# Attention of a soft mixture-of-experts kernel in 64x64 tiles of the matrix unit

## The chip, the cores and the metric

The kernel runs on one core of a Trainium2 chip. The metric is the device time of one execution in microseconds (us). Engines are named as the profile names them: PE is the matrix engine (PEld its weight loads), DVE the vector engine, ACT the scalar engine, POOL the general engine, SP the engine that only issues DMAs.

## The reference, cut to what matters

```python
def _attn_ref(q, k, v):                 # each (8, 12, 448, 64): batch, heads, tokens, head size
    scores = scale * np.matmul(q, k.transpose(0, 1, 3, 2))
    m = np.max(scores, axis=-1, keepdims=True)
    e = np.exp(scores - m)
    attn = e / (np.sum(e, axis=-1, keepdims=True) + np.exp(-m) + 1e-09)
    return np.matmul(attn, v)
...
def _moe_ref(x, phi, w1, w2):           # x (3584, 768); phi (768, 32); 8 experts of 768 x 1024 x 768
    logits = x @ phi
    d = softmax of logits over the rows; slot_input = d.T @ x
    slot_out = per expert: relu(slot_input[e] @ w1[e]) @ w2[e]
    c = softmax of logits over the slots
    return c @ slot_out
```

The first part is attention for 96 heads with one more term in the denominator, the second a soft mixture of experts over all 3584 rows that the attention gives.

## The kernel before, in words

The attention works on 48 pairs of heads (`NPAIR`), one after the other. A pair sits on the 128 partitions, 64 for each head. Six pairs are a batch element, three pairs a load group. Each pair goes through these steps; the line numbers are those of the profile.

- `load` (L168) brings q, k and v of three pairs with DMAs that POOL issues and that convert to bf16. q and k come with both heads on the partitions, one DMA each (L176). v comes in two DMAs (L180, L181), four of a partition's seven tokens each, so that one token is read twice, and `V` (L406) sorts it into place with four POOL copies.
- `T` (L241) turns q and k with 28 transposes of 64x64 (L256) into a PSUM bank of the pool psB; ACT (L263) or DVE (L265) copies the result.
- `A` (L274) makes the scores with queries as output rows, three chunks of 128 queries per head and a last chunk where the 64 remaining queries of both heads share a bank. DVE takes the maximum of each row (L287, L298, L307).
- `W1`, `W2`, `W3` (L310, L332, L340) turn the maxima of a group of three pairs into rows (`mT`): W1 writes the negated maxima on POOL, W2 are four products on PE, W3 copies the result with ACT and takes the exponential of the negated maximum.
- `Bk` (L352) makes the scores again, now with keys as output rows, adds the negated maxima by a product with a selection matrix, and ACT takes the exponential (L372, L402). In its mixed form it has one chunk of A woven in: a, b, b, bias, bias, a.
- `AV` (L421) multiplies by v, with a column of ones for the sum: per key chunk six products of 128x128 and two of 128x64, 65 columns each (L436), into one bank of the pool psV.
- `N1` (L443) evacuates that bank (ACT, L449), `N2` (L452) divides: two small operations on DVE (L464, L465), then three on POOL (L469, L479, L480).
- `PX` (L494) turns the pair's x with four 128x128 products (L501), ACT copies it (L507).
- `P` (L516) is the batch element's part of the mixture: logits, maxima, exponentials and the sums over the rows, in six steps that `post` spreads over the slots after the batch.

There are seven key chunks' worth of exponentials and seven reduces for a pair, each 128x448. The order is written out by hand: the program's order is the order of every engine's queue. The first pairs follow the list `ramp` (L716). Then the loop at L758 runs a slot for each pair in two halves (y = 0, 1): scores of pair s with the maxima of a later pair woven in, AV of pair s and s-1, turns of pair s+6, x of pair s-2. W1 is issued in the first half of every third slot (L805), ahead of the weight loads, and N2 of the pair before only in the second half (L803); W2 and W3 follow the turns in the second half (L783, L784). In the slots POOL also issues the loads of the experts' weights, half a matrix at a time (`load_half`, `half_at`), and later rows of them (`load_rows`, `stage_rows`).

PSUM has eight banks: three for A and P (psA), four for the scores of Bk, the turns and x (psB), one for AV (psV). After the attention come the experts' two products and the output, which the change hardly touches.

Of the kernel before, what the change touches and what calls it, by code (L numbers as in the profile page):

```python
# [24 lines left out]
HG = 6  # L25
NP = 3
W65 = 65
VS = 66
# [3 lines left out]
def kernel(  # L32
# [37 lines left out]
    ident2 = const.tile([128, 128], BF16, name="ident2")  # L70
    ones = const.tile([128, 2], BF16, name="ones")
    sel = const.tile([128, HG], BF16, name="sel")
    phi_sb = const.tile([128, KC, NS], BF16, name="phi_sb")
    halfm = const.tile([128, 2], F32, name="halfm")
    nhalfm = const.tile([128, 2], F32, name="nhalfm")
    band = const.tile([128, 4], BF16, name="band")

    NQK, NE, VPN, NATV = 7, 5, HG * 4 * VS, HG * 4 * D  # L80
    sizes = [("nq0", 2 * NP * S), ("nq1", 2 * NP * S), ("nv", NATV), ("qk6", 2 * S), ("wm1", 512),
             ("qk0", 2 * S), ("qk1", 2 * S), ("qk2", 2 * S), ("wm0", 512), ("xTa", 4 * 512), ("qk3", 2 * S),
             ("vp0", VPN), ("x0", 4 * DD), ("qk4", 2 * S), ("qk5", 2 * S), ("e2", NE * 2 * S), ("e1", S),
             ("vp1", VPN), ("xTb", 2 * 512), ("x1", 4 * DD)]
# [10 lines left out]
    e2_t = [part("e2", i * 2 * S, 2 * S).rearrange("p (h s) -> p h s", h=2) for i in range(NE)]  # L95
    e1_t = part("e1", 0, S)
    vp = [part(f"vp{i}", 0, VPN).rearrange("p (h i d) -> p h i d", h=HG, i=4) for i in range(2)]
    wm = [part(f"wm{i}", 0, 512).rearrange("p (i c) -> p i c", i=4) for i in range(2)]
# [57 lines left out]

    with ExitStack() as at:
# [4 lines left out]
        psB = pool("psB", 4, space=PSUM)  # L162
# [3 lines left out]
        ubuf = pu.tile([128, 2, 7 * W65], F32, name="ubuf")  # L166

        def load(g, nm, l0=0, l1=NP):  # L168


            b, h0 = g // 2, (g % 2) * HG
            src = {"q": q, "k": k, "v": v}[nm][b, h0:h0 + HG]
            if nm != "v":
                t = part(f"nq{g % 2}", "qk".index(nm) * NP * S, NP * S).rearrange("p (l x) -> p l x", l=NP)
                x = src.rearrange("(l h) (j t) d -> (h j) l (t d)", h=2, t=7)
                gdma(out=t[:, l0:l1, :], in_=x[:, l0:l1, :])  # L176
            else:
                t = part("nv", 0, NATV).rearrange("p (h t d) -> p h t d", h=HG, t=4)
                x = src.rearrange("h (p t) d -> p h t d", t=7)
                gdma(out=t[0:64], in_=x[:, :, 0:4, :])  # L180
                gdma(out=t[64:128], in_=x[:, :, 3:7, :])  # L181
            nat[nm, g] = t
# [3 lines left out]
        for a, src in enumerate((q, k)):  # L186
            nc.sync.dma_start(out=raw[:, a, :], in_=src[0, 0:2].rearrange("h (j t) d -> (h j) (t d)", t=7))
# [9 lines left out]
        for t in wm:  # L197
            nc.vector.memset(t, 0.0)

        def ones_in(t, eng):  # L200

            eng.memset(t, 0.0)
            eng.memset(t[:, :, 0:3, D:W65], 1.0)
            eng.memset(t[0:64, 0:HG:2, 3, D:W65], 1.0)
            eng.memset(t[64:128, 1:HG:2, 3, D:W65], 1.0)

        ones_in(vp[0], nc.vector)
        for t, x in ((halfm, 1.0), (nhalfm, -1.0)):
            nc.vector.memset(t, 0.0)
            for hl in range(2):  # L210
                nc.vector.memset(t[64 - 64 * hl:128 - 64 * hl, hl:hl + 1], x)
        nc.vector.memset(ones, 1.0)
        nc.vector.memset(ones[64:128, 1:2], 0.0)
# [4 lines left out]
        for h in range(2):  # L218
            nc.vector.tensor_add(ident2[:, 64 * h:64 * h + 64], ident[:, 0:64], ident[:, 64:128])
# [11 lines left out]
        mx, ngm, ec, mT, eT, av, us = {}, {}, {}, {}, {}, {}, {}  # L231
        qkT = {}
        st = {"e2": 0}


        def kcol(hl, tok):
            if hl == 0:
                return 384 if tok == 0 else (tok - 1) * 128 if tok < 4 else (tok - 4) * 128 + 64
            return tok * 128 if tok < 3 else (tok - 3) * 128 + 64 if tok < 6 else 384

        def T(n):  # L241
            g, pl = divmod(n, NP)
            first = n < NP * NP
            ps = psB.tile([128, 2, S], BF16, tag="b", name="ps_t")

            k0 = [psB.tile([128, 2, S], BF16, tag="b", name="ps_k") for _ in range(2)] if n == 0 else None
            for a in range(2):
                src = nat["qk"[a], g]
                order = [(tok, hl) for tok in range(7) for hl in range(2)]
                if a and n == 0:  # L250
                    order.sort(key=lambda z: kcol(z[1], z[0]))
                for tok, hl in order:
                    c = kcol(hl, tok) if a else (2 * tok if tok < 4 else 2 * tok - 7) * 64
                    r = slice(64 * hl, 64 * hl + 64)
                    o = k0[c // 256][r, 0, c:c + 64] if a and n == 0 else ps[r, a, c:c + 64]
                    nc.tensor.transpose(o, src[r, pl, tok * D:(tok + 1) * D], ident[r, r])  # L256
            t = qk_t[n % NQK]
            if n == 0:
                nc.scalar.copy(t[:, 0, :], ps[:, 0, :])
                nc.vector.tensor_copy(t[:, 1, 0:256], k0[0][:, 0, 0:256])  # L260
                nc.vector.tensor_copy(t[:, 1, 256:S], k0[1][:, 0, 256:S])
            elif first or n % 6 in (1, 3):
                nc.scalar.copy(t, ps)  # L263
            else:
                nc.vector.tensor_copy(t, ps)  # L265
            qkT[n] = t
# [5 lines left out]
        mg, mpl = (lambda n: group[n][0]), (lambda m: (0, (firsts + [NPAIR])[m + 1] - firsts[m]))  # L272

        def A(n, i, steps=False):  # L274
            g, pl = group[n]
            if g not in mx:
                mx[g] = psm.tile([128, 21], F32, tag="mx", name="mx")
            t = qkT[n]
            if steps:
                m = mx[g]  # L280

                def run(hl):
                    r = slice(64 * hl, 64 * hl + 64)
                    ps = psA.tile([128, 512], F32, tag="a", name="ps_a")
                    nc.tensor.matmul(ps[:, 0:S], t[r, 0, i * 128:(i + 1) * 128], t[r, 1, :], start=True, stop=True)  # L285
                    c = HG * i + 2 * pl + hl
                    nc.vector.reduce_max(m[:, c:c + 1], ps[:, 0:S], axis=AX.X)  # L287

                return [lambda: run(0), lambda: run(1)]
            if i < 3:  # L290
                pss = [psA.tile([128, 512], F32, tag="a", name="ps_a") for _ in range(2)]
                for hl in range(2):
                    r = slice(64 * hl, 64 * hl + 64)
                    nc.tensor.matmul(pss[hl][:, 0:S], t[r, 0, i * 128:(i + 1) * 128], t[r, 1, :],  # L294
                                     start=True, stop=True)
                for hl in range(2):
                    c = HG * i + 2 * pl + hl
                    nc.vector.reduce_max(mx[g][:, c:c + 1], pss[hl][:, 0:S], axis=AX.X)  # L298
            else:
                ps = psA.tile([128, 512], F32, tag="a", name="ps_a")  # L300

                for hl in range(2):
                    r = slice(64 * hl, 64 * hl + 64)
                    nc.tensor.matmul(ps[64 - 64 * hl:128 - 64 * hl, 0:S], t[r, 0, 384:448], t[r, 1, :],  # L304
                                     start=True, stop=True)
                c = 3 * HG + pl
                nc.vector.reduce_max(mx[g][:, c:c + 1], ps[:, 0:S], axis=AX.X)  # L307


        def W1(g):  # L310
            w, m = wm[g % 2], mx[g]
            l0, l1 = mpl(g)
            nm = psm.tile([128, 21], BF16, tag="ngm", name="ngm")
            neg = lambda o, s: nc.gpsimd.tensor_scalar(o, s, -1.0, None, op0=ALU.mult)
            cols = lambda t: t[:, 0:3 * HG].rearrange("p (i c) -> p i c", i=3)[:, :, 2 * l0:2 * l1]

            o = w[:, 3, :].rearrange("p (d c) -> p d c", d=2)[:, :, 2 * l0:2 * l1]
            nc.gpsimd.tensor_mul(
                o.rearrange("p d (l h) -> p d l h", h=2),
                m[:, 3 * HG + l0:3 * HG + l1].unsqueeze(1).unsqueeze(3).to_broadcast([128, 2, l1 - l0, 2]),  # L320
                nhalfm.unsqueeze(1).unsqueeze(1).to_broadcast([128, 2, l1 - l0, 2]))
            o = w[:, 0:3, :].rearrange("p i (d c) -> p i d c", d=2)[:, :, :, 2 * l0:2 * l1]
            neg(o, cols(m).unsqueeze(2).to_broadcast([128, 3, 2, 2 * (l1 - l0)]))
            if l1 - l0 == NP:
                neg(nm, m)
            else:
# [705 lines left out]
```

## Time and profile before

| what | value |
|---|---|
| median of 3 runs | 297.94 us (297.47 to 299.71) |
| the profiled execution, from first to last instruction | 299.0 us |
| mean granted PE clock | 0.956 (1.00 until 260 us) |
| PE, DVE, ACT, POOL busy in 60 to 80 us, of 20 us | 19.96, 19.60, 19.64, 16.44 |
| first and last of the products of PX | 32.8 us, 253.0 us |
| DMA share in 60 to 80 us | 1.15 |

The profiled execution's own time is its span: the page gives no time outside it. It is 1.1 us over the median. A busy time is the time in which at least one instruction of the engine was under way; instructions overlap, so the distance between starts says what one costs. A DMA share above 1 means that packets of the 16 engines overlap. The queue "instruction" in the list of DMA queues carries the program's own code to the engines.

### The profile page before, as it was taken

What the parts mean: (1) busy time and instruction counts of PE and PEld (TensorE: products, weight loads), DVE (VectorE), ACT (ScalarE), POOL (GpSimd) and SP (SyncE); (2) the same over time, 40 slices, a digit from 0 to 9 for tenths busy, and PEclk for the clock granted to TensorE, in tenths of its full rate; (3) what the DMA queues carried; (4) which work ended last, traced back from release to release, by engine and by line L of the source; (5) the groups of instructions that cost most, each with busy time, mean ns of one, the idle gap of its engine ahead of it and who ended that gap; (6) DMA issues with size and microseconds to landing.
All of it is one profiled execution on the core that took longest, in us unless ns stands there. A gap on an engine that the chain in (4) does not pass through costs nothing.

```text
span 299.0 us, 12398 instructions
## 1 busy us (share of the span) xinstructions
PE 271.4 (91%) x5174; PEld 162.5 (54%) x5174; DVE 249.7 (84%) x581; ACT 249.8 (84%) x559; POOL 195.9 (66%) x391
## 2 busy tenths in 40 slices
PE   5999899999999999999899999999999999996820
PEld 4445456566666566566556666656665555652100
DVE  5899799999999989999889999998999675537930
ACT  3569999999899989998989899989999987337820
POOL 8792887979696979887879697978686633000000
PEclk9999999999999999999999999999999999997555
DMA  7999998999999999999999999999799989908997
GB/s 132 147 143 208 149 138 138 188 165 188 185 204 179 184 176 202 163 182 182 202 159 184 176 199 152 196 183 196 125 150 187 213 185 263 344 10 318 380 453 322
DMA packets 47015, 58.67 MB, mean 196 GB/s; under 512 B 2800, under 2 KB 39920, under 8 KB 46704
## 3 DMA queue, kind: packets, MB, share of 16 engines
q0 software_dynamic: 40304, 42.29, 89.6%
q1 hardware_dynamic: 6656, 15.60, 13.8%
q8 instruction: 40, 0.66, 0.8%
q14 instruction: 15, 0.12, 0.1%
HBM read 89.16 MB, written 15.14 MB: 349 GB/s over the span
## 4 chain that ended last, share of the span: by engine, by line
PE 68%; ACT 10%; DVE 6%; POOL 6%; issue 4%; DMA 2%; DVEq 0%; POOLq 0%; ACTq 0%
PE ps_av L436 15%; PE ps_a L285 10%; PE ps_b L367 7%; PE ps_b L370 7%; PE ps_t L256 5%; PE ps_b L396 5%; PE ps_x L501 3%; PE ps_b L399 3%; ACT W L402 2%; PE ps_o L925 2%; DVE mx L298 2%; PE ps_s L623 2%; PE ps_h L862 2%; PE ps_so L882 2%; ACT W L263 2%
## 5 line engine op out<-in xcount | busy, mean ns | idle before, releaser
L287 DVE TENSOR_REDUCE mx<-ps_a 128x1 f32<-128x448 f32 x250 | 137.3, 613 | 4.6 <-PE ps_a L285 3.5
L372 ACT ACTIVATE W<-ps_b 128x448 bf16<-128x448 f32 x250 | 120.4, 574 | 0.0
L285 PE MATMUL ps_a<-W 64*128 64x448 bf16 x250 | 80.9, 352 | 0.0
L367 PE MATMUL ps_b<-W 64*128 64x448 bf16 x250 | 70.5, 352 | 1.1
L436 PE MATMUL ps_av<-W 128*128 128x65 bf16 (+1 forms) x1536 | 64.9, 196 | 2.2 <-issue 1.6
L436 PEld LDWEIGHTS <-W 128*128 128x128 bf16 (+1 forms) x1536 | 50.5, 100 | 30.2 <-issue 26.4
L370 PE MATMUL ps_b<-mT,sel 64*128 64x448 bf16 x250 | 66.5, 350 | 0.0
L469 POOL TENSOR_TENSOR W<-ubuf,rec 128x384 bf16<-128x384 f32 x44 | 36.3, 824 | 35.7 <-ACT W L507 19.3
L402 ACT ACTIVATE W<-ps_b 128x448 bf16<-128x448 f32 x86 | 46.1, 574 | 2.0 <-PE ps_b L399 2.0
L256 PEld LDWEIGHTS <-W 64*64 64x64 bf16 x1344 | 29.3, 112 | 12.7 <-issue 4.3
L507 ACT CAST W<-ps_x 128x512 bf16<-128x512 f32 x47 | 28.6, 608 | 7.4 <-PE ps_x L501 7.2
L256 PE MATMUL ps_t<-ident,W 64*64 64x64 bf16 x1330 | 30.6, 195 | 2.4 <-ACT W L215 1.4
L307 DVE TENSOR_REDUCE mx<-ps_a 128x1 f32<-128x448 f32 x48 | 29.5, 615 | 1.4 <-PE ps_a L304 1.4
L285 PEld LDWEIGHTS <-W 64*128 64x128 bf16 x250 | 23.4, 94 | 9.8
L114 POOL DMA_DIRECT2D W<-in_moe_w_dram x30 | 22.6, 755 | 7.9 <-PE ps_b L399 7.8
L370 PEld LDWEIGHTS <-sel 64*128 64x128 bf16 x250 | 19.6, 94 | 14.4 <-issue 5.6
L396 PE MATMUL ps_b<-W 64*64 64x448 bf16 (+1 forms) x134 | 27.1, 374 | 0.3
L449 ACT COPY ubuf<-ps_av 128x455 f32<-128x455 f32 x44 | 25.1, 571 | 0.8 <-POOL W L408 0.6
L399 PE MATMUL ps_b<-mT,sel 64*64 64x448 bf16 (+1 forms) x134 | 25.1, 354 | 0.1
L263 ACT COPY W<-ps_t 128x896 bf16<-128x896 bf16 x21 | 19.5, 927 | 6.5 <-PE ps_t L256 6.5
L298 DVE TENSOR_REDUCE mx<-ps_a 128x1 f32<-128x448 f32 x38 | 21.1, 616 | 1.9 <-PE ps_a L294 1.9
L480 POOL TENSOR_TENSOR W<-ubuf,rec 128x128 bf16<-128x128 f32 x44 | 17.5, 398 | 3.7
(156 smaller groups left out, 446.6 us busy)
## 6 DMA issues: line engine op xcount, KB each, us to landing
W<-in_moe_w_dram POOLq DMA_DIRECT2D x24, 768.0 KB, 9.9
W<-in_v_dram POOLq DMA_DIRECT2D x32, 192.0 KB, 6.5
out_dram<-W SPq DMA_DIRECT2D x2, 2688.0 KB, 10.0
W<-in_q_dram POOLq DMA_DIRECT2D x15, 336.0 KB, 6.3
W<-in_k_dram POOLq DMA_DIRECT2D x15, 336.0 KB, 7.5
stage<-in_moe_w_dram POOLq DMA_DIRECT2D x4, 768.0 KB, 9.6
W<-stage SPq DMA_DIRECT2D x4, 576.0 KB, 7.3
out_dram<-W SPq DMA_DIRECT2D x6, 384.0 KB, 3.0
```

What stands on the lines that cost most here:

```text
L256: nc.tensor.transpose(o, src[r, pl, tok * D:(tok + 1) * D], ident[r, r])
L285: nc.tensor.matmul(ps[:, 0:S], t[r, 0, i * 128:(i + 1) * 128], t[r, 1, :], start=True, stop=True)
L287: nc.vector.reduce_max(m[:, c:c + 1], ps[:, 0:S], axis=AX.X)
L307: nc.vector.reduce_max(mx[g][:, c:c + 1], ps[:, 0:S], axis=AX.X)
L367: nc.tensor.matmul(pss[hl][:, 0:S], t[rs[hl], 1, cols], t[rs[hl], 0, :], start=True, stop=False)
L370: nc.tensor.matmul(pss[hl][:, 0:S], sel[rs[hl], 2 * pl + hl:2 * pl + hl + 1].to_broadcast([64, 128]), mT[mg(n)][rs[hl], :], start=False, s ...
L372: nc.scalar.activation(e[:, hl, :], pss[hl][:, 0:S], AF.Exp, scale=scale)
L396: nc.tensor.matmul(outs[hl], t[rs[hl], 1, cols], t[rs[hl], 0, :], start=True, stop=False)
L399: nc.tensor.matmul(outs[hl], sel[rs[hl], 2 * pl + hl:2 * pl + hl + 1].to_broadcast([64, m]), mT[mg(n)][rs[hl], :], start=False, stop=True)
L402: nc.scalar.activation(e, p[:, 0:S], AF.Exp, scale=scale)
L436: nc.tensor.matmul(o, eT[n, i, hl][:, qc], vp[g % 2][:, 2 * pl + hl, i, 0:W65], start=(i == 0 and u == 0 and hl == 0) or (u == 3 and i == ...
L469: eng.tensor_mul(x[:, 0:3, c:c + 128].rearrange("p i (h d) -> p i h d", h=2), u[:, 0:6, 0:D].rearrange("p (i h) d -> p i h d", h=2), rec[: ...
```

## The change

All products of the attention take the form of 64x64 tiles, so that the two halves of the rows and the two halves of the columns of the matrix unit can hold four products at once.

- Seven chunks of 64 keys (or queries) per head in place of three of 128 and one of 64. `M` replaces A: two products, output halves swapped, one reduce. `R_` replaces Bk: two score products, then one M, then two bias products, then one exponential of both heads together. One bank per chunk; psB has three banks.
- `AV`: per key chunk 16 products of 64x64 with 65 columns, the eight with swapped halves first. The output takes two banks, the only buffer of psV.
- `TP` replaces T and PX: 16 turns of x and 28 of q and k, all 64x64, into that same buffer of psV; k is loaded with the heads' halves swapped, by two DMAs.
- `W2` makes 8 products of 64 columns, `W3` gets its exponentials from 4 more products on PE. W1 is two POOL products.
- v comes in one DMA per group and is copied by one POOL operation; N2 is one POOL product instead of three operations.
- A slot is one sequence of seven chunks, with AV of the pair before behind chunks 1 to 3, N1 at 3, N2 at 4, TP at 5. W1, W2, W3 stand at the end of chunks 4, 5 and 6 of every third slot.
- One of the logit products gets an extra one (`twin`) that masks a doubled half; the row counts of the late weight loads move by one.

```diff
-        psB = pool("psB", 4, space=PSUM)
+        psB = pool("psB", 3, space=PSUM)
...
+            if nm == "k":
+                for h in range(2):
+                    gdma(out=t[rs[1 - h], l0:l1, :], in_=x[h, :, l0:l1, :])
...
+        def TP(n=None, m=None):
+            ps = psV.tile([128, 2, 1024], BF16, tag="v", name="ps_t")
+            if m is not None:
+                b, pb = divmod(m, PB)
+                x, c = xb[b % 2], pb * 128
+                for i in range(4):
+                    for r in range(2):
+                        for h in range(2):
+                            nc.tensor.transpose(ps[rs[h], r, S + 64 * i:S + 64 * i + 64],
+                                                x[rs[r], i, c + 64 * h:c + 64 * h + 64], ident[rs[r], rs[r]])
+            if n is not None:
...
+                for t in range(NU):
+                    for hl in range(2):
+                        nc.tensor.transpose(ps[rs[hl], hl, qcol(t):qcol(t) + 64], sq[rs[hl], pl, t * D:t * D + D],
+                                            ident[rs[hl], rs[hl]])
+                    for hl in range(2):
+                        nc.tensor.transpose(ps[rs[hl], 1 - hl, t * 64:t * 64 + 64], sk[rs[1 - hl], pl, t * D:t * D + D],
+                                            ident[rs[1 - hl], rs[1 - hl]])
+            if m is not None:
+                nc.scalar.copy(xT(b, pb)..., ps[:, :, S:S + 256]...)
...
+        def M(mm=True):
...
+            t, ps = qkT[n], psA.tile([128, 512], F32, tag="a", name="ps_a")
+            def mms():
+                for hl in range(2):
+                    nc.tensor.matmul(ps[rs[1 - hl], 0:S], t[rs[hl], hl, u * 64:u * 64 + 64], t[rs[hl], 1 - hl, :],
+                                     start=True, stop=True)
+            def red():
+                c = NU * pl + u
+                nc.vector.reduce_max(mx[g][:, c:c + 1], ps[:, 0:S], axis=AX.X)
...
+        def R_(k):
+            n, c = divmod(k, NU)
+            t = qkT[n]
+            bank[k] = pb_("ps_b")
+            for hl in range(2):
+                nc.tensor.matmul(bank[k][rs[hl], 0:S], t[rs[hl], 1 - hl, c * 64:c * 64 + 64], t[rs[hl], hl, :],
+                                 start=True, stop=False)
+            m = M()
+            if m:
+                m[0]()
+                m[1]()
+            g, pl = group[n]
+            for hl in range(2):
+                nc.tensor.matmul(bank[k][rs[hl], 0:S], sel[rs[hl], 2 * pl + hl:2 * pl + hl + 1].to_broadcast([64, 64]),
+                                 mT[g][rs[hl], 0:S], start=False, stop=True)
+            eT[n, c] = e_t[k % NEB]
+            nc.scalar.activation(eT[n, c], bank.pop(k)[:, 0:S], AF.Exp, scale=scale)
...
         def W1(g):
+            L = size(g)
+            for d in range(2):
+                nc.gpsimd.tensor_mul(
+                    wm[:, :, 64 * d:64 * d + 2 * L].rearrange("p u (l h) -> p u l h", h=2),
+                    mx[g][:, 0:NU * L]..., nhalfm...)
         def W2(g):
+            ps = psA.tile([128, 512], F32, tag="a", name="ps_m")
+            for u in range(NU + 1):
+                nc.tensor.matmul(ps[:, u * 64:u * 64 + 64], wm[:, min(u, NU - 1), :], ident2, start=True, stop=True)
+            t = mT[g] = psm.tile([128, 512], BF16, tag="mT", name="mT")
+            nc.scalar.copy(t, ps)
         def W3(g):
+            ps = psA.tile([128, 4, HG], F32, tag="a", name="ps_e")
+            for i in range(4):
+                nc.tensor.matmul(ps[:, i, :], mT[g][:, i * 128:i * 128 + 128], ident[:, 0:HG], start=True, stop=True)
+            e = ec[g] = psm.tile([128, 4, HG], F32, tag="ec", name="ec", bufs=3)
+            nc.scalar.activation(e, ps, AF.Exp, scale=scale)
...
+        def AV(n, *cs):
+            g, pl = divmod(n, NP)
+            if 0 in cs:
+                av[n] = psV.tile([128, 2, 512], F32, tag="v", name="ps_av")
+            for c in cs:
+                for d in range(2):
+                    for i in range(4):
+                        for hl in range(2):
+                            z = 1 - hl if d == 0 else hl
+                            u = min(2 * i + z, NU - 1)
+                            nc.tensor.matmul(av[n][rs[z], hl, i * W65:i * W65 + W65], eT[n, c][rs[hl], u * 64:u * 64 + 64],
+                                             vp[g % 2][rs[hl], pl, c, 0:W65], start=(c == 0 and i == 0),
+                                             stop=(c == NU - 1), skip_group_check=True)
...
+        def slot(s, extra=()):
+            nonlocal rows
+            for c in range(NU):
+                R_(NU * s + c)
+                if c in (1, 2, 3) and s:
+                    AV(s - 1, *((0, 1), (2, 3), (4, 5, 6))[c - 1])
+                if c == 3:
+                    if s:
+                        N1(s - 1)
+                    for f in post.get(2 * s, ()):
+                        f()
+                if c == 4:
+                    if s:
+                        N2(s - 1)
+                    if wait_loads:
+                        f, z = wait_loads.pop()
+                        f(z)
+                    if s > 2:
+                        late_half(s)
+                    if 2 * s in rows_at:
+                        load_rows(rows, rows_at[2 * s])
+                        rows = rows_at[2 * s]
+                if c == 5 and s > 1:
+                    TP(s + 6 if s < NPAIR - 6 else None, s - 2)
+                if c == 6:
+                    for f in post.get(2 * s + 1, ()):
+                        f()
...
+                if s > 1 and s + 1 in firsts:
+                    if c == 4:
+                        W1(mg(s + 1))
+                    if c == 5:
                         W2(mg(s + 1))
+                    if c == 6:
                         W3(mg(s + 1))
```

`late_half` holds the weight loads of a slot; `rs` are the two halves of the partitions. The ramp becomes a short list of the same calls, and after the last slot come the turn of pair 46's x, the whole AV of pair 47, N1 and N2.

## The prediction

> **What bounds the kernel now.** I read the page first (busy shares, slices, queues, chain), then the groups of instructions kept apart by shape, then short windows of the timeline of PE and POOL, and the packed trace itself for the start of every instruction and of every packet.
>
> ```profile
> PE 271.4 (91%) x5174; PEld 162.5 (54%) x5174; DVE 249.7 (84%) x581; ACT 249.8 (84%) x559; POOL 195.9 (66%) x391
> ...
> PEclk9999999999999999999999999999999999997555
> DMA  7999998999999999999999999999799989908997
> ...
> q0 software_dynamic: 40304, 42.29, 89.6%
> ...
> q8 instruction: 40, 0.66, 0.8%
> ...
> PE 68%; ACT 10%; DVE 6%; POOL 6%; issue 4%; DMA 2%; DVEq 0%; POOLq 0%; ACTq 0%
> ```
>
> The attention runs from about 33.3 us, where the ramp ends, to 250.5 us: 45 slots of one head pair, 4.83 us each, 14.5 us for three (three, because the bias is made once in three slots). Starts counted between 61 and 228 us give per slot: ACT seven exponentials 0.425 apart, the evacuation 0.46, the copy of the turned x 0.49 and shares of the rest, about 4.55 us; DVE seven reduces 0.531 apart plus 0.9 of other work, about 4.6; PE 4.7 with hardly a gap. So three engines are full together, and the chain is mostly PE. The clock is full until 260 us. The DMA line says that the 16 engines have no slack either, and the last q8 line is the one that decides here: 40 packets of 16,384 bytes for 10,348 PE instructions (a weight load and a matmul each), one for every 256.
>
> ```profile
> 141.84 0.38 PE L396 MATMUL ps_b<-W 64*64 64x448 bf16 x2
> 141.85 0.38 PE L304 MATMUL ps_a<-W 64*64 64x448 bf16 x2
> 142.06 0.35 PE L399 MATMUL ps_b<-mT,sel 64*64 64x448 bf16 x2
> 142.25 0.41 PE L256 MATMUL ps_t<-ident,W 64*64 64x64 bf16 x16
> 143.26 0.38 PE L256 MATMUL ps_t<-ident,W 64*64 64x64 bf16 x12 [0.60 <-issue]
> ```
>
> Columns: start, length, engine and line, what ended the idle time. Two things are to be seen. First, the last key chunk already has the changed form: two ps_b and two ps_a products of 64x64 tiles start together and the next begins 0.21 us later, so four tiles do run at once. Second, PE stops in the middle of 28 turns for 0.60 us with nothing to wait for. The same happens at 148.9 us, and there a whole us is lost:
>
> ```profile
> 148.72 0.19 PE L337 MATMUL ps_m<-ident,W 128*128 128x64 bf16 x1
> 150.01 0.52 PE L436 MATMUL ps_av<-W 128*128 128x65 bf16 x12 [1.10 <-issue]
> ```
>
> Stops of this kind end at 143.26, 150.01, 164.05 and 201.96 us. Counted in PE instructions they lie at 5313, 5569, 6081 and 7617, exactly multiples of 256 apart, and each ends 2.32 to 2.47 us after a q8 packet began. So the packet that begins then is the code needed next, and it is usable 2.4 us after its start. No packet begins before PE has passed the edge of the block before: those between 57 and 235 us begin 0.9 to 4.4 us after it, 2.85 in the mean. Where queue 0 kept the engines a third busy (41.6, 47.5 us) or idle (262.7, 269.0) it was 0.3 to 0.5. Thus one block waits at a time, and 256 instructions need 2.85+2.45 = 5.3 us while loads are running, 2.8 without. Today 256 instructions last 6.3 us, so this shows only four times.
>
> **The change part by part.**
>
> *Instructions.* Per slot before: 24 score and bias products, 32 of AV, 28 turns, 4 of x = 88. After: 7 chunks x 6 = 42, AV 7 x 16 = 112, turns 28 + 16 = 44, together 198. For three slots add 12 for the bias (W2, W3) and 28 for the slots' work of a batch (56 in six slots): 634 matmuls, 1268 instructions, 4.95 blocks, where before there were 2.31.
>
> *PE's own work, three slots.* A 448-column product is followed after 0.189 us; a chunk is two such steps (scores with M, then bias): 21 x 0.378 = 7.9 us, against 2.43 a slot, 7.3, now. AV: 64x64 turns run two tiles at a time in 0.032, and the AV loop orders eight off-diagonal, then eight diagonal; the first eight lie beside the bias stream, so bursts of 2, 2 and 3 chunks add 0.32, 0.32 and 0.52: 3.5 us (now 1.03 a slot, 3.1). Turns: 44 at 0.008 if four tiles run like the scores (1.1 us) or 0.016 as now (2.1); I take the four-tile row, 1.1, against 2.6 now. W2 and W3: 12 at 0.03 plus four switches of tile form at 0.095 (last turn to AV: 0.125 less the 0.032 it takes) = 0.7. The batch work: 0.8 plus five pairs of switches over six slots, 0.5. Sum 14.5 us: the same as now. What is won in turns and switches is lost in scores and AV.
>
> *The wait of W2.* Before, W1 on POOL stands ahead of the slot's N2:
>
> ```profile
> 145.97 0.40 POOL L480 TENSOR_TENSOR W<-ubuf,rec 128x128 bf16<-128x128 f32 x1
> 146.33 0.21 POOL L318 TENSOR_TENSOR W<-mx,nhalfm 128x12 bf16<-128x12 f32 x1
> 146.97 0.31 POOL L314 TENSOR_SCALAR W<-mx 128x36 bf16<-128x36 f32 x1 [0.43 <-DVE mx L287]
> 147.25 0.28 POOL L314 TENSOR_SCALAR ngm<-mx 128x21 bf16<-128x21 f32 x1
> 147.47 0.84 POOL L114 DMA_DIRECT2D W<-in_moe_w_dram  x1
> ```
>
> It is done at 147.5 and PE takes it at 148.54. The N2 ahead of it belongs to an older pair, whose evacuation is long over. After, W1 is issued behind N2 of the pair whose AV has just ended and behind the weight load. From the end of AV: evacuation 0.17+0.57, DVE's two small ops to 1.3, one POOL product of 512 columns 1.05 (824 ns for 384, 398 for 128), the load 0.87 (not in two of 15 slots), W1 0.6: 3.1 or 4.0 us. PE has R4, R5 and the turns ahead of W2, 1.1 us, so W2 waits 2.0 to 2.9, and behind it the next chunk, then W3, another 0.35 for ACT's copy of the bias. Call it 3.0: PE's chain is 17.5 us for three slots.
>
> *Code.* Queue 0 has for three slots 768 packets of 88 ns (q, k), 384 of v (88 ns instead of 768 of 60: v is read once instead of with one token twice) and 768 of 173 ns of weights: 14.6 us over 16 engines, 12.2 at the 1.2 that a full slice shows. In those 12.2 us pass 12.2/5.3 = 2.3 blocks. The other 2.65 pass at PE's own pace, 14.5/4.95, about 3.0 each (above 2.8): 8.0. Together 20.2. The wait of W2 is mostly inside it, since code is fetched during it: a block that holds it lasts 6.0, which is 0.6 over 5.3, and 3.0 over a free one; as PE is late at W2 anyway, I add 0.6. So 20.8 us. Bounds: with a delay of 1.2 us the blocks fit under 17.5; with 4.3 (after the stops at 143.26 and 150.01 the next packets began 4.3 and 3.9 later) 21.6, and with the whole wait 24.
>
> *At nothing.* ACT's evacuation of 520 instead of 455 columns (+0.06 a slot), one exponential fewer per W3, DVE's 8 columns instead of 7, POOL's single N2 and V: ACT 13.8 and DVE 13.8 for three slots lie under 20.8. k's second DMA (0.75 on POOL) replaces v's. The single two-bank buffer that turns and AV share makes the turns wait for the evacuation (0 to 0.1 us) and AV for the copies (0 to 0.6 where ACT makes them): inside the wait for code, bare only if that goes.
>
> **Sum.** 15 x 20.8 = 312 for 217.5: +94.5. Ramp: 5.6 blocks instead of 2.6 in its 33 us, 5.6 x 5.3 = 30, nearly bare: +2. The last pair's AV stands whole behind the last slot: +1. The profiled execution spans 299.0; 396.5 on that footing, 395.4 on the median of 297.94 (1.1 less): **395 us**.
>
> **The rivals.** *Code stays hidden*, PE's chain alone counts: 15 x 17.5 = 262.5, +45 and +3: 346 us (320 to 360, by how much of W2's wait other work fills). For it: only four stops in 40 blocks; against: 5.3 is over 3.5, the time of a block then. The Trainium skill says just this (page "Runtime: NRT & Kernel Launch", section "Instruction fetch mechanics"): crossing a 16 KiB block costs little and is "mostly hidden". By that page this rival is the forecast; the four stops speak against it once blocks pass twice as fast.
>
> *W1 is early too*: the 14.5 us stand, with buffers that couple more tightly, 298 to 320.
>
> *Faster*: four tiles at 0.008 us each for AV as well and no wait at W2; then DVE's 13.8 us bind: 207 for 217.5, about 288. It decides only if a block passes in 13.8/4.95 = 2.8 us, which the trace shows only with the DMA idle.
>
> A rule against the whole idea is on the skill's page "TensorEngine Tiling (Array Packing)", "Gotcha 1: PSUM Pressure": row tiles can't use one PSUM bank at once. By it each chunk would take twice 0.378. The two L396 products do that, 3 ns apart, so the trace disagrees and it gets no chance.
>
> **How the numbers follow.** Bound by code 0.60 (360 to 440); code hidden, W2 waits 0.22; slower by less 0.06; within 1% 0.04; faster 0.08. One per cent is about what a measurement of this kernel can tell from no change. Range 320 to 440 leaves out the last three and a little above; its own range is 360 to 440. Slower 0.88, same 0.04, faster 0.08.
>
> **What would show it.** About 82 packets on q8; PE idle "issue" of some 60 us or more, its stops multiples of 256 instructions apart, ending 2.4 us after a packet begins; ACT and DVE near 65% busy; PE waiting for POOL at W2's line 1 to 3 us, 15 times; scores and M starting within 10 ns. I am wrong if stops come without regard to blocks, if packets begin under 1 us after the edge beside full DMA engines, or if PE shows no idle time and three slots still take 14 us.

## The result, and the profile after

The changed kernel takes 478.66 us (median of 4 runs, 476.27 to 482.28), the kernel before on the same chip 298.82 us (297.47 to 299.76): 1.6042 times as long, 95% interval 1.5948 to 1.6136. The profiled execution of the changed kernel spans 475.8 us. It is slower, as forecast, but by 180 us where 97 were forecast, and the time lies above the range of 320 to 440. Ratios, and the differences in us given with them, go by the executions within 1.5% of the fastest of their kernel; the profiled ones of two experiments, W1 ahead of N2 (451.17 us) and the divided AV products (463.57 us), lie above that, so that their groups read a little long.

The page of the changed kernel: busy times, granted clock and DMA share in 40 slices, two queues, and the chain that ended last.

```profile
PE 327.9 (69%) x10598; PEld 224.9 (47%) x10598; DVE 261.5 (55%) x567; ACT 271.4 (57%) x542; POOL 158.3 (33%) x233
...
PEclk9798888887778788977978787979989896899855
DMA  9978285573909476584909376676737592756696
...
q0 software_dynamic: 34320, 41.51, 55.3%
...
q8 instruction: 83, 1.36, 1.2%
...
PE 55%; issue 19%; ACT 9%; POOL 6%; DVE 6%; DMA 2%; POOLq 0%; ACTq 0%; DVEq 0%
```

There are 83 packets of code where there were 40, no engine is busy for more than 69% of the span, the chain holds 19% "issue" (4% before), and two things are new: the DMA line has holes (slices of 0, 2, 3) and the clock line is nowhere steadily full. One such hole from near, the timeline of PE (start, length, engine and line, in brackets the idle time before it and what ended it):

```profile
180.87 0.36 PE L313 MATMUL ps_b<-mT,sel 64*64 64x448 bf16 x2
180.89 0.72 PE L353 MATMUL ps_av<-W 64*64 64x65 bf16 x41
185.52 0.27 PE L353 MATMUL ps_av<-W 64*64 64x65 bf16 x3 [3.92 <-issue]
```

PE stops inside a burst of 48 AV products, 41 of them done and nothing in the profile that the next one waits for, for 3.92 us. The packet of code that comes just before the end of the stop began at 183.27, 2.25 us before it, and 4.22 us after PE had gone on from the stop before (179.05); in these 4.22 us queue 0 filled 0.93 of the 16 engines. Of the waits of PE, the two largest lines (us in total, times, longest):

```profile
PE ps_m L329 <- POOL W L321: 37.8, 16, 3.4
PE ps_av L353 <- issue: 30.8, 18, 3.9
```

L329 is W2 and L321 is W1. To put the span into terms I took the time from the first product of W2 in slot 2 to that in slot 44, 14 groups of three slots, and in it every moment in which PE neither computes nor loads weights, by what ended it ("code": ended by no releaser, over 0.15 us). All columns are us per group; the clock's share is half of the busy time that lies in stretches of granted clock 0.5.

| kernel | group | PE work at full clock | added by half clock | waits for code | wait of W2 | ACT, DVE | 256-instruction blocks |
|---|---|---|---|---|---|---|---|
| before | 14.6 | 14.3 | 0 | 0.18 | 0.04 | 0.08 | 2.24 |
| after | 25.9 | 14.5 | 3.6 | 4.84 | 2.51 | 0.49 | 4.89 |

All 33 stops of the code kind in the groups of the changed kernel have the same instruction number modulo 256, as the four before had, and end 2.2 to 3.0 us after a packet of code began.

### The profile page after: what moved, and what is told of

Its sections match the earlier page's. It is cut to its first block, busy times and chain, and to the rows that moved or that the text cites. A ratio compares the mean times of both kernels' runs of the same rounds, so it can differ in the third digit from the quotient of the medians.

```text
span 475.8 us, 23188 instructions
## 1 busy us (share of the span) xinstructions
PE 327.9 (69%) x10598; PEld 224.9 (47%) x10598; DVE 261.5 (55%) x567; ACT 271.4 (57%) x542; POOL 158.3 (33%) x233
## 4 chain that ended last, share of the span: by engine, by line
PE 55%; issue 19%; ACT 9%; POOL 6%; DVE 6%; DMA 2%; POOLq 0%; ACTq 0%; DVEq 0%
PE ps_av L353 17%; PE ps_b L305 11%; PE ps_b L313 8%; PE ps_a L285 6%; DVE mx L290 3%; ACT W L316 3%; POOL W L384 2%; PE ps_o L797 2%; DMA W<-in_k_dram 2%; PE ps_t L240 2%; ACT W L261 2%; POOL W L321 2%; PE ps_m L329 2%; ACT W L253 1%; PE ps_h L734 1%
## 5 line engine op out<-in xcount | busy, mean ns | idle before, releaser
L313 PE MATMUL ps_b<-mT,sel 64*64 64x448 bf16 x672 | 145.1, 415 | 9.5 <-issue 9.5
L305 PE MATMUL ps_b<-W 64*64 64x448 bf16 x672 | 145.3, 417 | 4.0 <-issue 4.0
L353 PE MATMUL ps_av<-W 64*64 64x65 bf16 x5376 | 118.9, 209 | 35.8 <-issue 30.8
L285 PE MATMUL ps_a<-W 64*64 64x448 bf16 x672 | 129.8, 429 | 8.5 <-issue 4.5
L353 PEld LDWEIGHTS <-W 64*64 64x64 bf16 x5376 | 106.6, 121 | 56.6 <-issue 46.9
L384 POOL TENSOR_TENSOR W<-ubuf,rec 128x512 bf16<-128x512 f32 x44 | 45.7, 1039 | 197.5 <-DVE rec L374 98.9
L305 PEld LDWEIGHTS <-W 64*64 64x64 bf16 x672 | 45.0, 120 | 25.8 <-issue 17.6
L285 PEld LDWEIGHTS <-W 64*64 64x64 bf16 x672 | 40.2, 112 | 21.6 <-issue 19.0
L313 PEld LDWEIGHTS <-sel 64*64 64x64 bf16 x672 | 44.6, 120 | 8.0 <-issue 2.7
L365 ACT COPY ubuf<-ps_av 128x520 f32<-128x520 f32 x44 | 26.0, 591 | 23.9 <-PE ps_av L353 23.4
L253 ACT COPY W<-ps_t 128x512 bf16<-128x512 bf16 x47 | 27.9, 593 | 17.7 <-PE ps_t L250 16.8
L329 PE MATMUL ps_m<-ident,W 128*128 128x64 bf16 x136 | 7.5, 202 | 38.0 <-POOL W L321 37.8
L240 PE MATMUL ps_t<-ident,W 64*64 64x64 bf16 x752 | 24.5, 206 | 10.1 <-issue 9.7
L240 PEld LDWEIGHTS <-W 64*64 64x64 bf16 x752 | 20.3, 114 | 22.4 <-issue 18.1
L250 PE MATMUL ps_t<-ident,W 64*64 64x64 bf16 x672 | 24.2, 208 | 8.9 <-issue 5.6
L247 PE MATMUL ps_t<-ident,W 64*64 64x64 bf16 x672 | 24.3, 207 | 6.4 <-issue 4.8
L263 DVE COPY W<-ps_t 128x896 bf16<-128x896 bf16 x26 | 16.2, 625 | 20.6 <-ACT W L253 20.2
L329 PEld LDWEIGHTS <-W 128*128 128x128 bf16 x136 | 5.4, 103 | 40.1 <-POOL W L321 40.1
```

The source lines that it names most:

```text
L240: nc.tensor.transpose(ps[rs[h], r, S + 64 * i:S + 64 * i + 64], x[rs[r], i, c + 64 * h:c + 64 * h + 64], ident[rs[r], rs[r]])
L247: nc.tensor.transpose(ps[rs[hl], hl, qcol(t):qcol(t) + 64], sq[rs[hl], pl, t * D:t * D + D], ident[rs[hl], rs[hl]])
L250: nc.tensor.transpose(ps[rs[hl], 1 - hl, t * 64:t * 64 + 64], sk[rs[1 - hl], pl, t * D:t * D + D], ident[rs[1 - hl], rs[1 - hl]])
L253: nc.scalar.copy(xT(b, pb).rearrange("p (i h j) -> p h i j", i=4, h=2), ps[:, :, S:S + 256].rearrange("p h (i j) -> p h i j", i=4))
L285: nc.tensor.matmul(ps[rs[1 - hl], 0:S], t[rs[hl], hl, u * 64:u * 64 + 64], t[rs[hl], 1 - hl, :], start=True, stop=True)
L305: nc.tensor.matmul(bank[k][rs[hl], 0:S], t[rs[hl], 1 - hl, c * 64:c * 64 + 64], t[rs[hl], hl, :], start=True, stop=False)
```

## The experiments

The theory at this point: a block of 256 PE instructions can't pass faster than its packet comes, the packet comes late while loads fill the DMA engines, and W2's wait stands on top. The rivals: that it is the half clock that costs the time, or that 64x64 tiles are slow in themselves. Each experiment starts from the changed kernel.

**W1 ahead of N2** (W2's wait taken away):

```diff
                 if c == 4:
+                    if s > 1 and s + 1 in firsts:
+                        W1(mg(s + 1))
                     if s:
                         N2(s - 1)
...
-                    if c == 4:
-                        W1(mg(s + 1))
```

> W1 is issued on POOL ahead of N2 and of the weight load; nothing else moves. In the changed kernel PE waits 2.65 us at W2 in every third slot. Theory A (the waits for code and for W2 add up, and after each the clock is halved for a while): the wait goes, 15 x 2.65 = 40 us, and some of the half-clock stretches with it: 425 to 440 us, granted clock above 0.84, PE idle at W2's line under 0.5 us each. Rival B (the wait lies inside the wait for code, as the prediction had it): at most 10 us, 468 to 479, the idle time turning up as waits for code.

445.74 us (442.6 to 451.2), ratio to the kernel before 1.4878 (1.4790 to 1.4966): 34 us less than the changed kernel, between the two expectations and nearer the first. W2's waits fell from 37.8 to 4.7 us; the largest line of waits for code stayed:

```profile
PE ps_av L353 <- issue: 30.0, 19, 4.0
...
PE ps_m L329 <- POOL W L321: 4.7, 12, 0.8
```

A group is 2.1 us shorter for 2.24 us less of this wait, but the other terms of the group moved too: all waits for code together rose from 4.84 to 5.61, the half clock's share fell from 3.6 to 2.3, and PE's work at full clock rose from 14.5 to 14.9. So a third of the wait (0.77 of 2.24) came back as waits for code; that the group gained nearly the whole wait comes, in this account, from the half clock that went with it.

**AV with wide weights** (AV alone back from 16 products of 64 queries to 8 of 128 per key chunk; the tiles are then 64x128, the count of PE instructions falls by a quarter; the mask of the doubled queries and the index of the output follow and are not shown):

```diff
-                for d in range(2):
-                    for i in range(4):
-                        for hl in range(2):
-                            z = 1 - hl if d == 0 else hl
-                            u = min(2 * i + z, NU - 1)
-                            nc.tensor.matmul(av[n][rs[z], hl, ...], eT[n, c][rs[hl], u * 64:u * 64 + 64], ...)
+                for i in range(4):
+                    for hl in range(2):
+                        q0 = min(i * 128, S - 128)
+                        nc.tensor.matmul(av[n][:, hl, ...], eT[n, c][rs[hl], q0:q0 + 128], ...)
```

> AV in 64x128 tiles: 56 products a slot instead of 112, the same sums; the doubled 64 queries of the last tile are others, and the mask and the output's index follow. Theory A (code is the limit): 932 instead of 1268 instructions in three slots, 1.3 blocks of 256 fewer at 3.4 us or more each, less idle time and less half clock: 25.9 us for three slots fall to 20 to 21, 390 to 410 us; q8 packets fall from 83 to about 63. Rival B (the smaller tiles are slow in themselves, by their work on PE): two row tiles instead of four tiles, 28 steps of 0.03 a slot for 37 and six switches of tile form: no change, 470 to 485.

420.48 us (417.1 to 422.8), ratio 1.4059 (1.3971 to 1.4147): 58 us less, where 69 to 89 were expected. From its page and its waits:

```profile
q8 instruction: 62, 1.02, 0.9%
```

```profile
PE ps_m L329 <- POOL W L321: 39.6, 16, 3.4
...
PE ps_av L351 <- issue: 3.5, 5, 1.1
```

With 3.58 blocks in a group the waits for code fall from 4.84 to 0.67, although PE's work rises to 15.7. W2's wait is about as it was (2.65), and the half clock still adds 2.0.

**Both:** the two edits together.

> W1 ahead of N2, and AV in 64x128 tiles. Theory A: both gains add, three slots take 17 to 18.5 us, 345 to 372 us, the granted clock above 0.93. Rival B (each hides the other): no better than the better one alone, 400 us or more.

380.46 us (379.1 to 382.2), ratio 1.2732 (1.2672 to 1.2793): 98 us less, where the two alone give 34 and 58. The two gains add, but the time is above the 345 to 372 expected: a group takes 19.3 us. The clock line of its page is all but full until the end of the attention:

```profile
PEclk9999999999999999999999999998999999989555
```

So the half clock follows the stops: the groups have 19 stops for code left, none over 1.6 us, and W2's waits are 0.8 us at most; the half clock then adds 0.2 us a group.

**PE kept busy while W2 waits** (12 products of 512 columns whose result is not used, ahead of W2's own):

```diff
+            for _ in range(12 if g > 1 else 0):
+                nc.tensor.matmul(ps, ident, w_sb["w1", 0][:, 0, 0:512], start=True, stop=True)
             for u in range(NU + 1):
```

> The changed kernel with 12 idle products of 512 columns issued ahead of W2's own (into the same bank, overwritten later), about 2.6 us at full clock, so that PE does not stand still while it waits for W1; it adds 24 instructions in three slots. Theory A (a stop of some 2.5 us halves the clock for one or two of its 3.4 us periods): the stretches at half clock behind W2 go, 1.7 to 3 us for three slots: 435 to 460 us, granted clock near 0.90. Rival B (the clock follows the load as a whole, not the stops): 479 to 490 us, clock as before, 0.84.

478.23 us (475.3 to 479.2), ratio 1.5983 (1.5904 to 1.6063): no different from the changed kernel. Neither expectation holds: the clock rose, the time did not fall. The dummies cost 2.7 us a group in place of a wait of 2.5; the mean clock in the groups rose from 0.843 to 0.881, which saves 0.9 us a group, and the waits for code took 0.3 of that back. So a quarter of the half clock's 3.6 us went, and the group came out 0.3 us shorter. What the other three quarters cost, this run does not show.

**Weights late** (the loads of the experts' weights moved behind the attention, so that q, k and v alone share the DMA engines with the code. The last rows of the weights land over the last batch's x, so what follows the attention computes on other data; only the groups are read):

```diff
-        half_at = {s: i + 1 for i, s in enumerate(range(4, 32, 3))}
+        half_at = {}
...
+        for i in range(1, 11):
+            load_half(i, 0, w_tile(i))
+            load_half(i, 1)
+        load_rows(0, 40)
```

> The changed kernel with all expert weights but the first half matrix loaded behind the attention, so its time as a whole is no measure (the loads then stand bare); three slots of the attention are, 25.9 us in the changed kernel. Theory A (code packets begin 3.5 us after they are due while the loads keep the DMA engines full, 1.1 us while these are idle): the full time for three slots shrinks from 12.2 to 5.2 us (q, k, v alone), 0.9 of 4.9 blocks pass in 5.95 us each and 4.0 in 3.5, 19.3 and W2's wait of 2.5: 21 to 23 us for three slots. Rival B (the loads do not matter, the distance from the edge to the packet is PE's own): 25 to 26.5.

One run, 506.71 us, no measure of the change: after the attention PE waits 85.8 us for the loads. In the attention a group takes 21.3 us instead of 25.9, within the 21 to 23 expected, with the same 4.89 blocks. Windows of 40 to 240 us of the changed kernel and of this one (length; PE, PEld, DVE, ACT, POOL busy and counts; clock; DMA share; GB/s):

```profile
40.00:240.00 200.00, 139.93 (x4812) 99.99 (x4812) 112.98 (x239) 117.37 (x238) 72.88 (x97) 0.83 0.61 100
```

```profile
40.00:240.00 200.00, 150.64 (x5702) 107.07 (x5704) 133.00 (x286) 139.85 (x288) 76.73 (x107) 0.92 0.36 51
```

In the same 200 us PE gets through 5702 matmuls instead of 4812. The waits for code fall from 4.84 to 1.95 a group, with the same program on PE: this is what ties the cost of code to the load on the DMA engines. Two other terms change with it: W2's falls to 1.6, with one load less ahead of W1 on POOL, and the half clock adds 1.6 instead of 3.6.

**Both, and the weights late.**

> W1 ahead of N2, AV in 64x128 tiles, and the weights behind the attention; three slots are the measure, 19.3 us with the weights in their place. Theory A: 3.6 blocks at 3.5 us are 12.5 us, below PE's own 16; the waits for code (1.25 us) all but go: 17.3 to 18.3 us. Rival B: 19 to 19.6, code waits as before.

One run, 458.57 us, read only in its groups, for the same reason. A group takes 18.0 us, within the 17.3 to 18.3 expected: PE's work 16.1, code 0.28, W2 0.41, ACT and DVE 1.16, at a granted clock of 1.00. This is the wide form with hardly a wait left, and it is still 3.4 us over the 14.6 before: wide AV raises PE's own work from 14.5 to 16.1. Neither form of AV, as run here, gains over the kernel before: one pays in instructions, the other in PE time.

**Both, with each AV product in two** (33 and 32 columns: 16 products per key chunk again, but 64x128 tiles):

```diff
+                        for z0, z1 in ((0, 33), (33, W65)):
-                        nc.tensor.matmul(av[n][:, hl, i * W65:i * W65 + W65], ...)
+                            nc.tensor.matmul(av[n][:, hl, i * W65 + z0:i * W65 + z1], ...)
```

> W1 ahead of N2, AV in 64x128 tiles, but each of AV's products split in its 33 first and 32 last columns: the same weights, columns and order, 112 products a slot again instead of 56, 1251 instructions for three slots instead of 915. Theory A (the number of instructions decides): 4.9 blocks, 2.05 of them at 5.95 us and the others at 3.5: 22 to 24 us for three slots in place of 19.3, 420 to 450 us, code idle time back at 4 to 6 us, clock below 0.92. Rival B (the work in the small tiles decides): at most 1 us more for three slots, 380 to 396.

461.24 us (454.6 to 466.5), ratio 1.5289 (1.5177 to 1.5402): 76 us more than both, and more than the 420 to 450 us expected. From its page:

```profile
PE 359.3 (78%) x10598; PEld 218.5 (47%) x10598; DVE 262.3 (57%) x567; ACT 274.1 (59%) x542; POOL 158.0 (34%) x233
...
PEclk9799797988889697969988698959898989878855
...
q8 instruction: 83, 1.36, 1.2%
```

With the same tiles and the same number of columns the group goes from 19.3 to 24.8 us: the waits for code from 1.25 to 3.86, the half clock's share from 0.2 to 2.9, PE's work at full clock from 16.2 to 17.1. So the count of instructions brings the stops and the half clock back with 64x128 tiles as well. That the half clock weighs so much here and could not be taken out by itself leaves open how the excess over the expectation divides between it and the code.

## Why the prediction was right in kind and too small

By place, on the profiled executions (475.8 us where 396.5 were forecast): the 14 groups took 158.7 us more than before where 14 x 6.3 = 88.2 were forecast, the way to W2 of slot 2 6.5 us more (38.6 against 32.0) where 2 were, and the rest 11.5 more where 6.3 + 1 were. The miss of 79 us is 70.5 + 4.5 + 4.2; nine tenths lie in the groups.

**PE's own work: right.** Forecast 14.5 us, measured 14.5 at full clock. The timeline of PE in the changed kernel shows its parts:

```profile
198.12 0.35 PE L313 MATMUL ps_b<-mT,sel 64*64 64x448 bf16 x2
198.13 0.60 PE L353 MATMUL ps_av<-W 64*64 64x65 bf16 x32
198.56 0.37 PE L285 MATMUL ps_a<-W 64*64 64x448 bf16 x1
198.56 0.35 PE L305 MATMUL ps_b<-W 64*64 64x448 bf16 x1
```

Scores and M start together, and 32 AV products take the time from 198.13 to 198.56, of which the bias stream takes 0.19: a burst adds 0.25 where 0.32 was forecast. Four turns in a row take 0.032 (0.008 each), as taken from the scores. That the sum is right is in part luck: put to the matmul that started last, the turns come to 1.7 us a group where 1.1 were forecast, and W2, W3 and the work of the batch to 1.4 where 2.0 were.

**Blocks of 256: right.** 83 packets on q8 against about 82, stops whole blocks apart.

**The delay of a packet: the first step that failed.** The 2.85 us of delay under load, and 0.35 without, were measured in the kernel before, mostly at blocks where PE was not stopped. Measured from where PE resumes after a stop to the start of the next packet, the changed kernel gives 3.5 us in the mean where queue 0 fills the engines until then (over 0.9 of them: 10 stops, 1.85 to 4.22, eight of them over 3.4), and 1.04 to 2.1, mostly 1.1, where it is idle (under 0.1: 17 stops). Of the 11 stops between, nine gave 1.06 to 1.25 us and two 4.05 and 4.09. With 2.45 to the use of the code a block takes 5.95 and 3.5 us, not 5.3 and 2.8. Packets in the groups are never less than 3.33 us apart (68 distances, a tenth below 3.42). The forecast let the blocks beside an idle queue pass in 3.0 us, faster than any block of these runs. The time for which loads fill the engines was right: queue 0 holds over 0.9 of them for 12.2 us a group. With the measured sizes the prediction's own sum reads 12.2/5.95 = 2.05 blocks under load and 2.84 x 3.5 = 9.9 us: 22.1 in place of 20.2. The kernel before could have shown it: after its four stops the next packets came 4.3, 3.9, 1.1 and 3.8 us later, 3.3 in the mean, and the prediction used the first two as a bound only.

**W2's wait: right in size, wrong in its place, the second step that failed.** Forecast 2.0 to 2.9 us; measured 1.6 to 3.4 in the groups, 2.5 in the mean. (The terms of the forecast add up to 2.95 and 3.8 us, not 3.1 and 4.0; that changes little.) POOL in the changed kernel, just as the forecast had it, product, load, W1 (start, length):

```profile
193.92 1.04 POOL L384 TENSOR_TENSOR W<-ubuf,rec 128x512 bf16<-128x512 f32 x1 [5.46 <-ACT W L316]
194.90 0.80 POOL L113 DMA_DIRECT2D W<-in_moe_w_dram  x1
195.73 0.48 POOL L321 TENSOR_TENSOR W<-mx,nhalfm 128x42 bf16<-128x42 f32 x2
```

PE takes it at 196.26 after 2.03 us. The prediction put this wait "mostly inside" the wait for code and added 0.6. W1 ahead of N2 made a group 2.1 us shorter, and only 0.77 of the 2.24 us taken away came back as waits for code. A reason that fits, but that no run tests by itself: the next packet begins only after PE has passed an edge, so a wait in the middle of a block also puts off the edge behind it.

**The half clock: put at nothing, and not foreseen.** In the groups of the changed kernel it lies in 25 stretches of 3.4, 6.8 and once 10.2 us; each begins during a stop of 1.4 to 3.9 us or within 2 us of its end. The Trainium skill, page "TensorE: Matmul & The Clock Gate", section "Part 1: The HAM clock gate", gives a window of 3413 ns and half speed after an idle one. The lengths of the stretches agree with that window, the condition does not: 20 of the 25 stops are shorter than it, and a stop of 3.63 us that ends at 333.61 has no half clock behind it. The half clock stretches PE's work by 3.6 us a group. How much of that it costs is open: the kernel that kept PE busy took 0.9 of it away, and of this 0.3 came back as waits for code. It can't be left out of the account: 22.1 + 2.5 for W2 + 0.5 for ACT and DVE is 25.1, and the 0.8 left of the measured 25.9 is not assigned by any run. By this sum the 5.1 us over the forecast of 20.8 are 1.9 of code, 1.9 of W2's wait, 0.5 of ACT and DVE and 0.8 open. How they divide between stops and half clock stays open too, since each experiment that took stops away took half clock with them.

**At nothing: nearly right.** ACT and DVE are at 57 and 55% (about 65% forecast, of a shorter time); PE waits 0.5 us a group for them.

**The rivals.** That code stays hidden (346 us) is refuted: 33 stops, 4.84 us of a group, and fewer of both in each kernel with fewer instructions or less DMA load. The page that says it, the Trainium skill's "Runtime: NRT & Kernel Launch", section "Instruction fetch mechanics" ("mostly hidden"), differs from what was measured here, and the measurement decides. That W1 is early too (298 to 320) did not happen; made so, the kernel still takes 445.74. Faster (288) did not happen either: even with hardly a wait a group of the wide form takes 18.0 us, and PE's work alone in the 64x64 form, 14.5, is what the whole group took before.

## What to carry to other kernels

Count the instructions of an engine, not only its columns: on PE a weight load and a matmul are two, and here the packets for 256 of them came no less than 3.3 us apart, and some 6 us apart, by the sizes above, while loads filled the DMA engines. Small tiles that run four at a time cost nothing in PE time here, and yet the kernel is 1.6 times as long: with more than twice the instructions PE stops for code, the clock halves behind the stops, and the new order on POOL adds a wait. When you take a delay from a kernel that rarely shows it, take it from the places that resemble the new state (here the stops), and do not let one wait cover another that lies at a different place of a block without a run that shows it.

## What was not expected of the hardware

- The next packet of code begins mostly 1.1 us after PE resumes from a stop with queue 0 idle, and 3.5 us in the mean (to 4.2) with it full; how the load delays it no run shows.
- After the packet's start it takes 2.2 to 3.0 us until PE goes on, at every stop in the groups of the changed kernel.
- The half clock of the groups came with stops of 1.4 to 3.9 us, not with each of them, and lasted 3.4, 6.8 or 10.2 us.
- Splitting each AV product in two (the same columns and tiles) adds 0.9 us a group to PE's work at full clock and 5.5 us to the group.
